# The bias row of a fused attention and MLP kernel as one matmul in place of three

## The chip, the cores and the metric

The kernel runs on one core of one Trainium2 chip. The metric is the device time of one execution in microseconds (us). Times are given as the median of several runs. One more execution is recorded by the hardware profiler, and the numbers about single instructions come from that one.

## The reference

Two stages are computed. The first is a gated linear attention over 4 batches, 8 heads, 768 steps and a head width of 48: a state is decayed, a product of key and value is added, and the query reads it. The second is an MLP with a squared ReLU over the 3072 rows of 384 that come out of it.

```python
for t in range(S):
    state = alpha[:, :, t, :, None] * state + einsum('bhd,bhe->bhde', k[:, :, t], v[:, :, t])
    y[:, :, t] = einsum('bhd,bhde->bhe', q[:, :, t], state)
x = y.transpose(0, 2, 1, 3).reshape(B * S, H * D)
h = x @ w_in                       # 384 -> 2048
r = maximum(h, 0.0)
g = s * (r * r) + b
out = g @ w_out                    # 2048 -> 384
```

Since `b` is one number, `b` times the column sums of `w_out` is the same row for all 3072 outputs. This is the bias row: 384 numbers, which are added to each row of `(s * r * r) @ w_out`.

## The kernel before

The 3072 rows are cut into 24 blocks of 128 (`n` from 0 to 23, six for each batch). For each block the kernel forms the decays (`ln`, `cum_pe`, `cum_act`), scales queries and keys (`qb_mul`, `kb_mul`), transposes them (`tr`, `qk_copy`), forms the scores (`amat`) and masks them (`mask`), and forms the attention's output (`y_pe`, `y_act`). It carries the state on with `pst_pe`, `t1` and `sd`. The output is transposed (`xt_pe`, `xt_act`), goes through the first matrix in four quarters (`mp`, with `rl` and `sq` behind each), and through the second, again in four quarters (`o_pe`, then `o_out`). Matmul inputs are bf16; sums are fp32.

The program is straight-line code. Each step is an event with a position on a scale of 8 per block; events are sorted by position and issued in that order. Each engine takes its own instructions in this order, and a semaphore holds an instruction back until what it needs is there. The position thus sets the order in each engine's queue and not a time.

PSUM, where matmuls put their results, has eight banks, and each is one tile here: `ct_ps`, two `a_ps`, `y_ps`, `p_ps`, two `h_ps` and `o_ps`. The output of the attention takes columns 0 to 383 of `y_ps`; the state's product takes columns 0 to 383 of `p_ps`. From block 11 on, the scores of odd blocks are written into all 512 columns of `y_ps` and `p_ps`, those of even blocks into the two `a_ps`.

The bias row is made in three steps. `colsum` adds up the pieces of `w_out` on VectorE (up to position 101.3), and `bias_sum` folds the two halves of that into `cs_sb[:, 0]`, 128 partitions by 384 columns (position 103.3). `bias_row` then sums over the partitions: a matmul with a matrix of ones in fp32 puts the same sums into all 128 partitions, and a ScalarE activation scales them by `b` and puts them into `bias_w`. Before the change this is done for 128 columns at a time: part 0 goes into columns 384 to 511 of `y_ps` at position 105.5, part 1 into the same columns of `p_ps` at 105.6, and part 2 again into `y_ps` at 121.5.

The events around positions 105.5 and 121.5, in their order:

```
103.9   y_pe 13, pst_pe 13, y_act 13        119.9   y_pe 15, pst_pe 15, y_act 15
104.05  o_pe 12 (quarter 0)                 120.05  o_pe 14 (quarter 0)
104.74  tr 15                               120.74  tr 17
104.95  t1 13, sd 13                        120.95  t1 15, sd 15
105.5   bias_row part 0 (y_ps)              121.5   bias_row part 2 (y_ps)
105.6   bias_row part 1 (p_ps)
105.65  o_pe 12 (quarter 1)                 121.65  o_pe 14 (quarter 1)
105.71  qk_copy 15                          121.71  qk_copy 17
105.89  xt_pe 13, xt_act 13                 121.89  xt_pe 15, xt_act 15
106.17  amat 14, then amat 15 (106.35)      122.17  amat 16, then amat 17 (122.35)
```

`bias_w` is first read at position 125.3. The results of the first 14 blocks are kept in SBUF until then (`o_out` puts them into `keep_sb`, and `add_bias` adds the row later); those of later blocks get it as they leave PSUM.

The lines of the profile for these steps: L210 and L211 are matmul and activation of `bias_row`, L206 is `bias_sum`, L329 the transposes, L341 their copy, L362 the scores, L371 the masks, L467 and L476 the attention's output, L498 its evacuation, L489 the state's product and L550 (or L548) `t1`, L528 and L535 the transposed output and its copy, L574 the first matrix, L587 and L594 ReLU and square, L605 the second matrix.

Of the kernel before, what the change touches and what calls it, by code (L numbers as in the profile page):

```python
# [10 lines left out]
AF = mybir.ActivationFunctionType  # L11
# [3 lines left out]
def kernel(  # L15
# [12 lines left out]
    nc = tc.nc  # L28
# [28 lines left out]
    y_ps = ps.tile([128, 512], FP32, name="y_ps")  # L57
    p_ps = ps.tile([128, 512], FP32, name="p_ps")
# [19 lines left out]
    ones_f = sb.tile([128, 128], FP32, name="ones_f")  # L78
    sb_row = sb.tile([1, 2], FP32, name="sb_row")
    sb_col = sb.tile([128, 2], FP32, name="sb_col")  # L80
    s_col, b_col = sb_col[:, 0:1], sb_col[:, 1:2]
# [36 lines left out]
    cs_sb = sb.tile([128, 2, d_model], FP32, name="cs_sb")  # L118
    bias_w = sb.tile([128, d_model], FP32, name="bias_w")
# [85 lines left out]
    def bias_sum():  # L205
        nc.vector.tensor_tensor(out=cs_sb[:, 0], in0=cs_sb[:, 0], in1=cs_sb[:, 1], op=ALU.add)  # L206

    def bias_row(i):
        part, c = (y_ps, p_ps, y_ps)[i][:, 384:512], slice(128 * i, 128 * i + 128)
        nc.tensor.matmul(out=part, lhsT=ones_f, rhs=cs_sb[:, 0, c], start=True, stop=True)  # L210
        nc.scalar.activation(out=bias_w[:, c], in_=part, func=AF.Copy, scale=b_col)  # L211

    def spread():
        nc.tensor.matmul(out=p_ps[:, 510:512], lhsT=ones_f[0:1], rhs=sb_row, start=True, stop=True)
# [489 lines left out]
    for s in range(2):  # L704
        nc.vector.memset(mask_p[s], 0.0)
        for b in range(2):
            part = mask_p[s][64 * b : 64 * b + 64]
            nc.gpsimd.affine_select(
                out=part,
                in_=part,  # L710
# [17 lines left out]
    def at(pos, fn, *args):  # L728
        events.append((pos, len(events), fn, args))
# [55 lines left out]
    for i in range(3, 8):  # L785
        at(69.3 + 8 * (i - 3), colsum, i)
    at(103.3, bias_sum)
    for i in range(3):
        at((105.5, 105.6, 121.5)[i], bias_row, i)
    for n in range(NKEEP):  # L790
        at(125.3 + 4.55 * n, add_bias, n)
        at(126.2 + 4.55 * n, store, n, keep_sb[n])
# [15 lines left out]
    for n in range(4, NBLK):  # L808
        p = 8 * n
        f = max(0.0, min((n - 5) / 3.0, 1.0))  # L810
        c, t, a = 9.0 + 5.8 * f, 5.8 + 5.0 * f, 3.4 + 4.5 * f
# [59 lines left out]
```

## Time and profile before

| | |
|---|---|
| median of 3 runs | 185.96 us (185.91 to 186.97) |
| profiled execution: time, span | 186.9 us, 185.1 us |
| mean granted TensorE clock | 0.991 |
| TensorE matmul busy | 178.9 us, 97% of the span |
| VectorE busy | 142.4 us, 77% |
| ScalarE busy | 122.8 us, 66% |
| GpSimd busy | 58.9 us, 32% |

The span is what the profiler sees from the first to the last instruction; 1.8 us of the profiled execution lie around it. In the rows of the profile, PE is TensorE's matmuls and PEld its weight loads, DVE is VectorE, ACT ScalarE, POOL GpSimd, and SPq the queue from which SyncE issues transfers. L210 is line 210 of the kernel. A row names the tile that is written, then those that are read (`out<-in`), with the numbers of ring buffers left out. Matmuls overlap: a record's end includes the tail of the pipeline, so the distance between the starts of two matmuls, and not the duration of one, is what a matmul takes of the array's time. The chain is followed back from the last instruction to what released each step; its pieces do not overlap.

### The profile page before, as it was taken

To read this page: it belongs to the slowest core of one execution; us is meant where nothing else is said; L and a number is where in the kernel's file an instruction comes from. 1 tells how busy PE (TensorE), PEld (TensorE's weight loads), DVE (VectorE), ACT (ScalarE), POOL (GpSimd) and SP (SyncE) were. 2 spreads that over 40 slices of the span, in tenths; PEclk is the share of its full clock that TensorE was granted. 3 is DMA by queue.
4 is the path that set the end of the run, shared out by engine and by line. 5 is a ranking of instruction groups with operands and counts; after the bars stand their busy time and mean duration, and the time that the engine had idled before them with its cause. 6 is when DMAs were issued, how large, how long until landed. Compare 5 with 4: busy or idle time off the path is not lost.

```text
span 185.1 us, 6233 instructions
## 1 busy us (share of the span) xinstructions
PE 178.9 (97%) x2510; PEld 143.7 (78%) x2510; DVE 142.4 (77%) x301; ACT 122.8 (66%) x255; POOL 58.9 (32%) x97
## 2 busy tenths in 40 slices
PE   7988999999999999999999999999999999999993
PEld 2556999866698777787888778878878878878893
DVE  7688878866657588987888976689789799886541
ACT  3885897976678957656766756856746746734750
POOL 7437470011330625042505343242202442333000
PEclk9996999999999999999999999999999999999999
DMA  5998989989478989892976563934896944224212
GB/s 155 312 317 307 270 235 387 317 158 208 76 153 151 211 163 189 165 175 43 172 138 123 104 121 78 192 74 124 157 207 142 189 135 132 66 66 149 65 52 76
DMA packets 105262, 30.33 MB, mean 164 GB/s; under 512 B 98435, under 2 KB 103698, under 8 KB 105234
## 3 DMA queue, kind: packets, MB, share of 16 engines
q1 hardware_dynamic: 105230, 29.94, 69.5%
q8 instruction: 19, 0.31, 0.7%
q14 instruction: 9, 0.07, 0.1%
q10 hardware_dynamic: 4, 0.00, 0.0%
HBM read 25.19 MB, written 4.74 MB: 162 GB/s over the span
## 4 chain that ended last, share of the span: by engine, by line
PE 83%; DMA 4%; DVE 3%; ACT 3%; SPq 2%; issue 1%; POOL 1%; ACTq 0%; POOLq 0%; DVEq 0%
PE h_ps L574 27%; PE o_ps L605 26%; PE ct_ps L329 4%; PE h_ps L605 3%; DMA al_sb<-in_alpha_dram 3%; PE a_ps L574 2%; PE a_ps L362 2%; PE y_ps L476 2%; PE ct_ps L574 2%; SPq L152 2%; PE h_ps L528 2%; DMA v_sb<-in_v_dram 2%; PE o_ps L574 2%; PE ct_ps L256 1%; PE a_ps L631 1%
## 5 line engine op out<-in xcount | busy, mean ns | idle before, releaser
L574 PEld LDWEIGHTS <-w_in_bf 128*128 128x128 bf16 x1152 | 67.5, 98 | 4.4 <-issue 0.2
L587 ACT ACTIVATE r_sb<-h_ps 128x512 bf16<-128x512 f32 x79 | 46.9, 603 | 30.7 <-PE h_ps L574 29.0
L605 PE MATMUL o_ps<-w_out_bf,gt_all 128*128 128x384 bf16 x320 | 64.0, 326 | 0.0
L574 PE MATMUL h_ps<-xd_all,w_in_bf 128*128 128x128 bf16 x948 | 60.3, 219 | 0.0
L560 POOL TENSOR_TENSOR sd_sb<-t_sb,blast 48x192 bf16<-48x192 f32 x40 | 25.7, 642 | 86.2 <-DVE t_sb L550 58.8
L594 DVE TENSOR_TENSOR gt_all<-r_sb 128x512 bf16<-128x512 bf16 x96 | 40.7, 441 | 15.8 <-ACT r_sb L587 15.6
L605 PEld LDWEIGHTS <-gt_all 128*128 128x128 bf16 x368 | 32.6, 98 | 15.3
L251 POOL CAST v_bf<-v_sb 128x384 bf16<-128x384 f32 x23 | 14.6, 646 | 23.5 <-DMA v_sb<-in_v_dram 21.4
L318 DVE TENSOR_TENSOR kb_sb<-k_sb,bi_sb 128x384 bf16<-128x384 f32 x24 | 14.5, 605 | 7.4 <-ACT bi_sb L269 7.4
L321 DVE TENSOR_TENSOR qb_sb<-q_sb,b_sb 128x384 bf16<-128x384 f32 x24 | 13.5, 564 | 2.1 <-ACT b_sb L270 1.6
L535 ACT ACTIVATE xd_all<-h_ps 128x384 bf16<-128x384 bf16 x19 | 9.5, 502 | 8.0 <-PE h_ps L528 7.9
L564 POOL TENSOR_TENSOR sc_sb<-t_sb,blast 112x384 f32<-112x384 f32 x16 | 14.3, 895 | 1.3
L240 ACT ACTIVATE la_sb<-al_sb 128x384 bf16<-128x384 f32 x24 | 12.5, 529 | 2.7 <-DVE blast L721 2.3
L498 ACT ACTIVATE y_bf<-y_ps 128x384 bf16<-128x384 f32 x22 | 10.9, 498 | 3.5 <-PE y_ps L476 3.1
L371 DVE TENSOR_TENSOR am_a<-a_ps,mask 128x512 bf16<-128x512 f32 x13 | 8.9, 687 | 5.0 <-PE a_ps L362 4.9
L341 DVE COPY qkT<-ct_ps 112x1024 bf16<-112x1024 bf16 x16 | 11.0, 685 | 2.3 <-PE ct_ps L329 2.1
L329 PEld LDWEIGHTS <-qb_sb 128*112 128x112 bf16 x96 | 8.3, 133 | 4.0 <-DVE qb_sb L321 2.5
L269 ACT ACTIVATE bi_sb<-ct_ps 128x384 f32<-128x384 f32 x19 | 9.3, 489 | 2.1 <-PE ct_ps L256 2.0
L371 DVE TENSOR_TENSOR am_b<-a_ps,mask 128x512 bf16<-128x512 f32 x13 | 8.9, 682 | 1.7 <-PE a_ps L362 1.7
L270 ACT ACTIVATE b_sb<-ct_ps 128x384 f32<-128x384 f32 x19 | 9.4, 497 | 0.0
L656 DVE TENSOR_TENSOR w_in_st<-w_in_st,bias_w 128x384 f32<-128x384 f32 x14 | 8.3, 593 | 0.0
L329 PEld LDWEIGHTS <-kb_sb 128*112 128x112 bf16 x96 | 7.4, 133 | 0.7 <-DVE kb_sb L318 0.2
(145 smaller groups left out, 256.9 us busy)
## 6 DMA issues: line engine op xcount, KB each, us to landing
al_sb<-in_alpha_dram SPq DMA_DIRECT2D x20, 192.0 KB, 2.9
q_sb<-in_q_dram SPq DMA_DIRECT2D x20, 192.0 KB, 4.2
k_sb<-in_k_dram SPq DMA_DIRECT2D x20, 192.0 KB, 8.1
v_sb<-in_v_dram SPq DMA_DIRECT2D x20, 192.0 KB, 3.6
w_in_st<-in_moe_w_in_dram SPq DMA_DIRECT2D x4, 768.0 KB
w_out_st<-in_moe_w_out_dram SPq DMA_DIRECT2D x4, 768.0 KB
out_dram<-w_in_st SPq DMA_DIRECT2D x10, 192.0 KB
out_dram<-out_sb SPq DMA_DIRECT2D x5, 192.0 KB, 2.2
```

The costliest lines, as they stand in the source:

```text
L240: nc.scalar.activation(out=la_sb[n % 2][:, :, 0:48], in_=raw("al", n), func=AF.Ln)
L251: nc.gpsimd.tensor_copy(out=v_bf[n % 4], in_=raw("v", n))
L318: nc.vector.tensor_tensor(out=kb_sb[n % 4][:, :, 0:48], in0=raw("k", n), in1=bi_sb[n % 2], op=ALU.mult)
L321: nc.vector.tensor_tensor(out=qb_sb[n % 2][:, :, 0:48], in0=raw("q", n), in1=b_sb[n % 3], op=ALU.mult)
L329: nc.tensor.transpose(out=t_bank(n, x if n in pair_of else None)[0:112, x, p, :], in_=t.rearrange("a h d -> a (h d)")[:, 128 * p : 128 * p ...
L371: nc.vector.tensor_tensor(out=am_sb[e][n % 2], in0=a_bank(n)[e], in1=mask4, op=ALU.mult)
L560: nc.gpsimd.tensor_tensor(out=sd[r, :, d], in0=t1_sb[r, :, d], in1=bl[r].to_broadcast([48, NP, 48]), op=ALU.mult)
L564: nc.gpsimd.tensor_tensor(out=sc_sb[0:112], in0=t1_sb[0:112], in1=bl[0:112].to_broadcast([112, NP, 96]), op=ALU.mult)
L574: nc.tensor.matmul(out=hp[:, jj * C : (jj + 1) * C], lhsT=w_in_bf[:, kk, 128 * j : 128 * (j + 1)], rhs=xd_sb[n][:, kk], start=(kk == 0), s ...
L587: nc.scalar.activation(out=rs, in_=room((g, u)), func=AF.Relu)
L594: nc.vector.tensor_tensor(out=gt_sb[g][:, u * 512 : (u + 1) * 512], in0=rs, in1=rs, op=ALU.mult)
L605: nc.tensor.matmul(out=op[:, 0:d_model], lhsT=gt_sb[n][:, j * C : (j + 1) * C], rhs=w_out_bf[:, j, :], start=(j == 0), stop=(j == NJ - 1),)
```

## The change

The sums over the partitions are formed by one matmul of 384 columns into columns 0 to 383 of `y_ps`, the place of the attention's output, and one activation takes them to `bias_w`. It stands at position 105.5; the events at 105.6 and 121.5 are gone.

```diff
-    def bias_row(i):
-        part, c = (y_ps, p_ps, y_ps)[i][:, 384:512], slice(128 * i, 128 * i + 128)
-        nc.tensor.matmul(out=part, lhsT=ones_f, rhs=cs_sb[:, 0, c], start=True, stop=True)
-        nc.scalar.activation(out=bias_w[:, c], in_=part, func=AF.Copy, scale=b_col)
+    def bias_row():
+        nc.tensor.matmul(out=y_ps[:, 0:384], lhsT=ones_f, rhs=cs_sb[:, 0], start=True, stop=True)
+        nc.scalar.activation(out=bias_w, in_=y_ps[:, 0:384], func=AF.Copy, scale=b_col)
...
     at(103.3, bias_sum)
-    for i in range(3):
-        at((105.5, 105.6, 121.5)[i], bias_row, i)
+    at(105.5, bias_row)
```

## The prediction

> **What bounds the kernel now.** I read the page first: the share of each engine, the granted clock, and the chain that ended last.
>
> ```profile
> span 185.1 us, 6233 instructions
> PE 178.9 (97%) x2510; PEld 143.7 (78%) x2510; DVE 142.4 (77%) x301; ACT 122.8 (66%) x255; POOL 58.9 (32%) x97
> PEclk9996999999999999999999999999999999999999
> PE 83%; DMA 4%; DVE 3%; ACT 3%; SPq 2%; issue 1%; POOL 1%; ACTq 0%; POOLq 0%; DVEq 0%
> ```
>
> TensorE is busy for 97% of the span, holds 83% of the chain, and runs at full clock in every slice but one early on. The change lies after 104 us, so the question is whether TensorE waits for anything between there and the end. Next I read the table of waits, for TensorE's matmuls and then for its weight loads, from 106 us to the end.
>
> ```profile
> PE p_ps L210 <- DVE t_sb L550: 0.3, 1, 0.3
> ...
> PEld p_ps L210 <- DVE t_sb L550: 0.5, 1, 0.5
> PEld L329 <- DVE qb_sb L321: 0.3, 1, 0.3
> ```
>
> The columns are total us, times, longest us. In 80 us the matmul side waits once, and that wait belongs to the code being changed: the second part of the bias row (L210, into `p_ps`) waits for VectorE's state sum `t1` (L550), which reads the other columns of the same bank. The wait is thus kept for the bank, not for the columns. Everything else arrives in time, so an instruction taken from TensorE's queue here should bring the end forward by the time it held the queue.
>
> **The change part by part.** The timeline around 105.5 us has all of the first two parts. Columns are start, duration, engine, line, operation, and in brackets the idle time before with what ended it.
>
> ```profile
> 105.24 0.39 PE L329 MATMUL ct_ps<-ident,kb_sb 128*112 128x128 bf16 x4
> 105.41 0.30 PEld L210 LDWEIGHTS y_ps<-cs_sb,ones_f 128*128 128x128 f32 x2
> 105.47 0.44 PE L210 MATMUL y_ps<-cs_sb,ones_f 128*128 128x128 f32 x2
> 105.63 0.55 DVE L550 TENSOR_TENSOR t_sb<-p_ps,sc_sb 112x384 f32<-112x384 f32 x1
> 105.94 0.37 ACT L211 ACTIVATE bias_w<-y_ps,sb_col 128x128 f32<-128x128 f32 x1 [0.80 <-PE y_ps L210]
> 106.10 0.68 DVE L341 COPY qkT<-ct_ps 112x1024 bf16<-112x1024 bf16 x1
> 106.23 0.49 PE L210 MATMUL p_ps<-cs_sb,ones_f 128*128 128x128 f32 x2 [0.33 <-DVE t_sb L550]
> 106.56 0.81 PE L605 MATMUL o_ps<-w_out_bf,gt_all 128*128 128x384 bf16 x4
> 107.58 0.49 ACT L535 ACTIVATE xd_all<-h_ps 128x384 bf16<-128x384 bf16 x1 [0.45 <-PE h_ps L528]
> 107.70 0.22 PE L362 MATMUL y_ps<-qkT 48*128 48x128 bf16 x1
> ```
>
> One fp32 matmul of the source is two instructions. The output product behind both parts (L605) starts at 106.56, which is 106.56 - 105.47 = 1.09 us after the first part began.
>
> The third part stands alone, without a stall. The chain in order of time gives its cost (start, length, what):
>
> ```profile
> 120.14 0.45 PE ct_ps L329 x8
> 120.58 0.28 PE y_ps L210 x2
> 120.86 0.65 PE o_ps L605 x4
> ...
> 122.99 1.34 PE h_ps L574 x24
> ```
>
> It holds 0.28 us of the chain, with TensorE's work packed on both sides. All of that goes: **-0.28 us**. Three parts at this price are 0.84 us, and the stall is what else the 1.09 us holds, 1.09 - 0.56 = 0.53 us by starts (the table shows 0.3 for the matmuls, because a record's end includes the tail that the next matmul overlaps, and 0.5 for the weight loads).
>
> What is added is an fp32 matmul of 384 columns, of which the trace has none. Its nearest rows are the 128-column calls:
>
> ```profile
> L210 PEld LDWEIGHTS y_ps<-cs_sb,ones_f x4: 190/191/192, 105.4 to 120.5; 128*128 128x128 f32 x4
> L210 PE MATMUL y_ps<-cs_sb,ones_f x4: 275/302/328, 105.5 to 120.6; 128*128 128x128 f32 x4
> L210 PE MATMUL p_ps<-cs_sb,ones_f x2: 275/326/377, 106.2 to 106.4; 128*128 128x128 f32 x2
> ```
>
> The second instruction of the `p_ps` call ends at 106.23 + 0.49 = 106.72 and lasts 0.275, so it starts at 106.445, and the next matmul starts at 106.56: a pass over 128 columns holds the array for 0.115 us. A bf16 matmul of 128 columns takes 1.34/24 = 0.056 us of the chain (L574), so fp32 costs twice that per pass. The bf16 matmul of 384 columns takes 0.65/4 = 0.1625 us (L605). Two fp32 passes over 384 columns should then take 2 x 2 x 0.1625 = **0.65 us**. The first pass of a 128-column call is longer, 0.28 - 0.115 = 0.165 us, which I put down to the second weight load (0.19 us); behind a first pass of 0.325 us that load is covered. The bounds are the bf16 rate below, 2 x 0.1625 = 0.33 us, and three calls above, 0.84 us. I take 0.65, since it has the measured fp32 rate and the measured width.
>
> The output product then starts at 105.47 + 0.65 = 106.12 instead of 106.56: **-0.44 us**. The bounds make it -0.76 to -0.25.
>
> The Trainium skill, "TensorE: Matmul & The Clock Gate", section "Back-to-back issue gap", gives a warm matmul N/2.4 + 2.5 ns, and "Perfetto Trace Analysis", section "Engine Utilization", halves the output rate for the fp32 low-high form. An estimate from both pages is 2 x (320 + 2.5) = 645 ns for the wide call and 6 x (107 + 2.5) = 657 ns for the three narrow ones. By that rule the merging alone is worth 12 ns, and nearly the whole gain would be the stall, about 0.5 us in all. The trace agrees for the second pass (115 ns against 109) and not for the first (165 ns); the measured 0.28 a call decides.
>
> ScalarE's side: three activations of 0.367 us become one over 384 columns. Widening it is priced by two PSUM readers of ScalarE:
>
> ```profile
> L211 ACT ACTIVATE bias_w<-y_ps,sb_col x2: 367/367/367, 105.9 to 120.9; 128x128 f32<-128x128 f32 x2
> ...
> L587 ACT ACTIVATE r_sb<-h_ps 128x512 bf16<-128x512 f32 x68 | 40.6, 604 | 30.4 <-PE h_ps L574 28.8
> ...
> L498 ACT ACTIVATE y_bf<-y_ps 128x384 bf16<-128x384 f32 x16 | 8.0, 501 | 1.7 <-PE y_ps L476 1.7
> ```
>
> 128 more columns cost 604 - 501 = 103 ns, so the new one takes 367 + 2 x 103 = 573 ns (between 0.49, the narrower price of L498, and 3 x 0.367 = 1.10). Nothing on the path pays for it: ScalarE sits idle 0.80 us before the first part, and behind it in its queue is the copy of the transposed block (L535), which waits for TensorE in any case.
>
> **What the wide evacuation can hold up.** The next writer of the bank of `y` is the score product of the following block (L362 into `y_ps`, 107.70, about 107.26 after the change). The wide matmul ends with its tail of 0.16 us (0.275 - 0.115) at 106.28, ScalarE starts 0.03 later as it does now (105.91 to 105.94), and ends near 106.88. That leaves about 0.4 us, less the handoff. If the matmul takes longer, writer and reader move together; only an activation beyond about 0.95 us would reach the score product, so its upper bound of 1.10 would cost 0.15 us. The other input of that product, VectorE's copy (L341), ends at 106.78: 0.48 us early. The `t1` for which the second part waited ends at 106.18, and its next user on TensorE, the score product into `p_ps`, comes at about 107.27. So the stall has no successor. In front of the new matmul nothing new is waited for: it needs the evacuation of `y` and the sum of the bias, as the first part did, and that part started right behind the transposes (L329). No DMA is added or moved, and the queues of SP and POOL are passed by nothing.
>
> **Sum.** -0.44 - 0.28 = -0.72 us, with bounds -1.04 and -0.53. Against the profiled execution that is a span of 185.1 - 0.7 = 184.4 us and a time of 186.9 - 0.7 = 186.2 us. The profiled execution is 0.9 us above the median of the runs (185.96, from 185.91 to 186.97), so the same difference put on the median gives **185.25 us**, own range 184.9 to 185.45.
>
> **Rivals.**
>
> *The gain is taken back later.* TensorE arrives earlier everywhere behind 106 us, and VectorE is nearly full: in the stretch from 150 to 170 us it is busy 18.29 of 20 us.
>
> ```profile
> 150.00:170.00 20.00, 20.00 (x286) 16.56 (x285) 18.29 (x38) 11.69 (x24) 6.84 (x10) 1.00 0.30 89
> ```
>
> At one place the chain already shows the seam:
>
> ```profile
> 107.87 0.05 PE y_ps L362
> ...
> 149.49 0.18 PE y_ps L362
> ```
>
> It takes 0.18 us there against 0.05 at 107.87, and VectorE's copy for that block (L341 below) ends just then, at 148.71 + 0.68 = 149.39. If VectorE's pace were its own, TensorE would wait 0.72 us longer at that seam and the kernel would end at 185.96. Against it: VectorE's unbroken run up to that copy begins with a wait for ScalarE, which waited for TensorE.
>
> ```profile
> 144.61 0.45 DVE L594 TENSOR_TENSOR gt_all<-r_sb 128x512 bf16<-128x512 bf16 x1 [1.08 <-ACT r_sb L587]
> 145.28 0.42 DVE L594 TENSOR_TENSOR gt_all<-r_sb 128x512 bf16<-128x512 bf16 x1 [0.22 <-ACT r_sb L587]
> ...
> 148.71 0.68 DVE L341 COPY qkT<-ct_ps 112x1024 bf16<-112x1024 bf16 x1
> ```
>
> So the run starts earlier when TensorE does. Half a loss would be 185.6. Chance 0.18 for 185.45 to 185.96.
>
> *The change does not do what it says: the merged matmul is no cheaper than three.* Then the call takes 0.84, the output product starts at 106.31, and the sum is -0.25 - 0.28 = -0.53: 185.43, the upper edge of the forecast. If the score product also met the late evacuation (0.15), it is 185.6. By the rule of the Trainium skill above the time would lie here as well, at 185.96 - 0.5 = 185.46. Chance 0.08.
>
> *Slower: a wide fp32 pass doesn't overlap.* If each 128 columns of a pass cost their whole record of 0.275 us, the wide call would hold TensorE from 105.47 for 6 x 0.275 = 1.65 us. The output product would start at 107.12, 0.56 us later than before; with the third part's 0.28 gone that is +0.28, or 186.24. It decides from a call of 0.65 + 0.72 = 1.37 us on. The 0.115 us from a second pass to the next matmul, seen twice, speaks against it. Chance 0.06.
>
> **How the numbers follow.** The forecast has 0.68, the rivals 0.18, 0.08 and 0.06. The range of 184.9 to 186.1 reaches from the lower bound of the forecast over the whole of the first two rivals, with a little room above for scatter, and leaves out most of the slower one. A measurement of this kernel can tell about 1% from no change, which is 184.1 or 187.8 us. None of the cases reaches either; I leave 0.04 on each side for what I have not seen, and 0.92 for within 1%.
>
> **What would show it.** On the changed kernel's timeline: two fp32 matmul instructions of 384 columns from about 105.5 us, with the output product (L605) 0.65 us behind the first; no wait for `t_sb` among TensorE's; one activation of about 0.57 us, over before the score product into `y_ps`; no fp32 matmul near 120 us; and the same step of the chain 0.44 us earlier at 107 us and 0.72 us earlier from 121 us to the end. The prediction is wrong if that lead shrinks on the way, which would put the seam at the place where it shrinks, or if the wide call's two instructions start more than 0.4 us apart.

## The result and the profile after

| | before | after |
|---|---|---|
| median of 22 runs each, side by side | 186.39 us | 185.85 us |
| ratio | | 0.996, 95% interval 0.9944 to 0.9976 |
| span of the profiled execution | 185.1 us | 183.9 us |
| TensorE matmul busy | 178.9 us | 177.7 us |

The ratio is a gain of 0.75 us (0.45 to 1.04) on 186.39; -0.72 had been forecast. The two medians lie only 0.54 us apart; four runs of before are above 187.5 us and no run of after is above 186.24. The gain is clear of no change and well under 1%. The forecast of 185.25 was put on a median of three runs; the median of 22 runs of before is 0.43 us higher, and this, more than the change, is why the time itself lies 0.6 us above the forecast. That is outside the forecast's own range (184.9 to 185.45) and in the stretch that the first rival had claimed, although what that rival tells of did not happen.

The two spans differ by 1.2 us, more than the change gave. The table of stretches shows why. Columns are the stretch, its length, busy time and count of PE, PEld, DVE, ACT and POOL, the granted clock, and the share and rate of DMA. The first fence is before, the second after.

```profile
0.00:20.00 20.00, 17.16 (x230) 11.04 (x231) 15.81 (x46) 13.21 (x32) 10.71 (x27) 0.91 0.95 281
```

```profile
0.00:20.00 20.00, 16.90 (x242) 10.67 (x243) 16.89 (x46) 13.96 (x34) 10.91 (x28) 1.00 1.00 293
```

In the profiled execution of before, the clock was 0.91 in the first 20 us, where the two programs are alike. I therefore measure from an instruction ahead of the change: the **tail** runs from the state's part of `y` of block 13 to VectorE's last instruction. (The expectations below call this the end of that instruction; all their numbers, and mine here, take its start.) Its two ends before and, in the second fence, after:

```profile
103.83 0.34 PE L467 MATMUL y_ps<-sd_sb,qkT 112*128 112x96 bf16 x4
...
182.29 0.36 DVE L640 TENSOR_TENSOR out_sb<-a_ps,bias_w 128x192 f32<-128x192 f32 x1 [0.30 <-PE a_ps L631]
```

```profile
103.27 0.34 PE L466 MATMUL y_ps<-sd_sb,qkT 112*128 112x96 bf16 x4
...
181.06 0.36 DVE L639 TENSOR_TENSOR out_sb<-a_ps,bias_w 128x192 f32<-128x192 f32 x1 [0.30 <-PE a_ps L630]
```

The tail is 182.29 - 103.83 = 78.46 us before and 181.06 - 103.27 = 77.79 after, so the change itself is worth **-0.67 us** in the trace. Another 0.56 us of the difference of the spans lies ahead of the tail (103.83 against 103.27). The timeline of after around the new matmul (lines of the kernel are one lower than before from L209 on):

```profile
104.85 0.30 PEld L209 LDWEIGHTS y_ps<-cs_sb,ones_f 128*128 128x128 f32 x2
104.91 0.86 PE L209 MATMUL y_ps<-cs_sb,ones_f 128*128 128x384 f32 x2
105.54 0.68 DVE L340 COPY qkT<-ct_ps 112x1024 bf16<-112x1024 bf16 x1
105.61 0.81 PE L604 MATMUL o_ps<-w_out_bf,gt_all 128*128 128x384 bf16 x4
105.81 0.58 ACT L210 ACTIVATE bias_w<-y_ps,sb_col 128x384 f32<-128x384 f32 x1 [1.23 <-PE y_ps L209]
106.75 0.22 PE L361 MATMUL y_ps<-qkT 48*128 48x128 bf16 x1
```

The **call**, from the start of the first bias matmul to the start of the output product behind it, takes 105.61 - 104.91 = 0.70 us; before it was 1.09 with the stall. Among TensorE's waits from 100 us on, `t_sb` is gone. What is left is the wait for `qb_sb`, which was there before, and an idle of the weight loads with no releaser:

```profile
PEld L328 <- DVE qb_sb L320: 0.3, 1, 0.3
PEld L604 <- issue: 0.2, 1, 0.2
```

In the chain, the transposes at the old place of part 2 are followed directly by the output product:

```profile
119.19 0.45 PE ct_ps L328 x8
119.63 0.65 PE o_ps L604 x4
...
148.27 0.18 PE y_ps L361
```

The lead against before, counted from the start of the tail, is 0.39 us at the scores of block 15 (107.70 - 103.83 against 106.75 - 103.27). It is 0.67 behind the old place of part 2, and the same 0.67 at the end. The seam near 149 us is still 0.18 us long.

### The profile page after: what moved, and what is told of

Same layout as the page of the kernel before. It is cut to its first block, busy times and chain, and to the rows that moved or that the text cites. A ratio compares the mean times of both kernels' runs of the same rounds, so it can differ in the third digit from the quotient of the medians.

```text
span 183.9 us, 6223 instructions
## 1 busy us (share of the span) xinstructions
PE 177.7 (97%) x2506; PEld 142.3 (77%) x2506; DVE 143.4 (78%) x301; ACT 122.6 (67%) x253; POOL 60.3 (33%) x97
## 4 chain that ended last, share of the span: by engine, by line
PE 90%; ACT 4%; DVE 3%; issue 1%; POOL 1%; ACTq 0%; POOLq 0%; DVEq 0%
PE h_ps L573 29%; PE o_ps L604 28%; PE ct_ps L328 5%; PE h_ps L604 3%; PE a_ps L573 2%; PE a_ps L361 2%; PE o_ps L229 2%; PE y_ps L475 2%; PE ct_ps L573 2%; PE h_ps L527 2%; PE ct_ps L255 2%; PE o_ps L573 2%; PE y_ps L466 1%; PE a_ps L630 1%; PE a_ps L604 1%; PE p_ps L488 1%
## 5 line engine op out<-in xcount | busy, mean ns | idle before, releaser
L559 POOL TENSOR_TENSOR sd_sb<-t_sb,blast 48x192 bf16<-48x192 f32 x40 | 26.9, 672 | 85.8 <-DVE t_sb L549 57.8
L250 POOL CAST v_bf<-v_sb 128x384 bf16<-128x384 f32 x23 | 15.4, 678 | 21.2 <-DMA v_sb<-in_v_dram 19.2
L563 POOL TENSOR_TENSOR sc_sb<-t_sb,blast 112x384 f32<-112x384 f32 x16 | 13.8, 864 | 1.3
```

The source lines that it names most:

```text
L250: nc.gpsimd.tensor_copy(out=v_bf[n % 4], in_=raw("v", n))
L559: nc.gpsimd.tensor_tensor(out=sd[r, :, d], in0=t1_sb[r, :, d], in1=bl[r].to_broadcast([48, NP, 48]), op=ALU.mult)
L563: nc.gpsimd.tensor_tensor(out=sc_sb[0:112], in0=t1_sb[0:112], in1=bl[0:112].to_broadcast([112, NP, 96]), op=ALU.mult)
```

## Experiments

Each kernel was timed beside the kernel before, in runs of the same chip; ratios are to those. The tail and the call are read from each trace. They are the finer measure: an interval of a ratio is about 0.2% to either side, or 0.4 us. A tail comes from one execution, and how far it scatters from one to the next was not measured; but what each trace below shows around the bias row, calls and waits, adds up to the change of its tail within 0.03 us.

**Three narrow matmuls at one place.** It isolates the width.

```diff
-        nc.tensor.matmul(out=y_ps[:, 0:384], lhsT=ones_f, rhs=cs_sb[:, 0], start=True, stop=True)
+        for i in range(3):
+            c = slice(128 * i, 128 * i + 128)
+            nc.tensor.matmul(out=y_ps[:, c], lhsT=ones_f, rhs=cs_sb[:, 0, c], start=True, stop=True)
```

> The place and the single activation of the changed kernel, but three matmuls of 128 columns side by side in the bank of y in place of the wide one. It isolates the width. Two distances are read from the trace: the call, from the start of the first bias matmul to the start of the output product behind it (1.09 us before, with the stall; 0.70 after), and the tail, from the start of the state's part of y of block 13 to the end of VectorE's last instruction (182.29 - 103.83 = 78.46 us before, 181.06 - 103.27 = 77.79 after). My prediction's price of 0.28 us a call makes the call 3 x 0.28 = 0.84 and the tail 77.93. A rival reading of the changed kernel's trace is that only the first weight load of the whole row is exposed (0.05 us) and each narrow pass costs 0.115: call 6 x 0.115 + 0.05 = 0.74, tail 77.83. By the rule of the back-to-back gap the call is 0.66 to 0.71 and the tail as after.

The grouped rows of this kernel's bias line, and its timeline:

```profile
L211 PEld LDWEIGHTS y_ps<-cs_sb,ones_f x6: 190/192/192, 105.1 to 105.7; 128*128 128x128 f32 x6
L211 PE MATMUL y_ps<-cs_sb,ones_f x6: 275/275/328, 105.2 to 105.8; 128*128 128x128 f32 x6
...
105.19 0.89 PE L211 MATMUL y_ps<-cs_sb,ones_f 128*128 128x128 f32 x6
...
105.91 0.81 PE L606 MATMUL o_ps<-w_out_bf,gt_all 128*128 128x384 bf16 x4
```

The ends of its tail:

```profile
103.55 0.34 PE L468 MATMUL y_ps<-sd_sb,qkT 112*128 112x96 bf16 x4
...
181.37 0.36 DVE L641 TENSOR_TENSOR out_sb<-a_ps,bias_w 128x192 f32<-128x192 f32 x1 [0.30 <-PE a_ps L632]
```

The call takes 105.91 - 105.19 = 0.72 us, and the tail 181.37 - 103.55 = 77.82. The ratio is 0.9975 (0.9957 to 0.9994). Only the first of the six records is longer than 275 ns. So the width is worth 0.02 to 0.03 us: three narrow matmuls in a row cost 0.72 and not 3 x 0.28 = 0.84. The price of 0.28 belongs to a call that stands alone behind the transposes.

**The stall alone.** The kernel before, with part 1 behind the next quarter of the output product.

```diff
-        at((105.5, 105.6, 121.5)[i], bias_row, i)
+        at((105.5, 105.66, 121.5)[i], bias_row, i)
```

> The kernel before, with part 1 of the bias row one event later, behind the second quarter of the output product of block 12, so that the state sum it waits for is done. It isolates the stall. My theory: the stall of 0.53 us goes with nothing in its place but a short wait of the scores of block 15 for the later evacuation of that part (0 to 0.15 us): tail 77.93 to 78.08 against 78.46, ratio to before 0.997 to 0.998. Rival, the gain of the change comes from the merging and not from the stall: tail about 78.4.

In this execution the tail begins at 107.20. The granted clock was 1.00 throughout it.

```profile
107.20 0.34 PE L467 MATMUL y_ps<-sd_sb,qkT 112*128 112x96 bf16 x4
...
110.19 0.37 ACT L211 ACTIVATE bias_w<-p_ps,sb_col 128x128 f32<-128x128 f32 x1 [0.50 <-PE p_ps L210]
110.49 0.22 PE L362 MATMUL y_ps<-qkT 48*128 48x128 bf16 x1
110.61 0.21 PE L362 MATMUL p_ps<-qkT 48*128 48x128 bf16 x1
...
185.19 0.36 DVE L640 TENSOR_TENSOR out_sb<-a_ps,bias_w 128x192 f32<-128x192 f32 x1 [0.30 <-PE a_ps L631]
```

The tail is 77.99 us, 0.47 less than before; the ratio is 0.9977 (0.9954 to 1.0), whose interval just reaches no change. One event's place gives 0.47 of the 0.67 us, with nothing merged. A little of the stall comes back as the short wait that was expected: the score product into `p_ps` starts 0.12 us behind its neighbour and not 0.01 as before, when the activation that reads this bank is done (110.19 + 0.37 = 110.56).

**The wide matmul in the other bank.** `p_ps` in place of `y_ps`.

```diff
-        nc.tensor.matmul(out=y_ps[:, 0:384], lhsT=ones_f, rhs=cs_sb[:, 0], start=True, stop=True)
-        nc.scalar.activation(out=bias_w, in_=y_ps[:, 0:384], func=AF.Copy, scale=b_col)
+        nc.tensor.matmul(out=p_ps[:, 0:384], lhsT=ones_f, rhs=cs_sb[:, 0], start=True, stop=True)
+        nc.scalar.activation(out=bias_w, in_=p_ps[:, 0:384], func=AF.Copy, scale=b_col)
```

> The changed kernel with the wide matmul in the bank of the state's product in place of the bank of y. It isolates the choice of the bank. My theory: TensorE waits for the state sum of block 13 as part 1 did, 0.76 us behind the point at which the matmul could start; the call costs 0.70 as after, and the tail is 77.79 + 0.76 = 78.55 us, 0.1 us longer than before. Rival, the merging is what gains: tail 77.8.

```profile
106.72 0.91 PE L209 MATMUL p_ps<-cs_sb,ones_f 128*128 128x384 f32 x2 [0.60 <-DVE t_sb L549]
...
107.47 0.81 PE L604 MATMUL o_ps<-w_out_bf,gt_all 128*128 128x384 bf16 x4
```

The ends of its tail:

```profile
104.31 0.34 PE L466 MATMUL y_ps<-sd_sb,qkT 112*128 112x96 bf16 x4
...
182.93 0.36 DVE L639 TENSOR_TENSOR out_sb<-a_ps,bias_w 128x192 f32<-128x192 f32 x1 [0.30 <-PE a_ps L630]
```

The wait is back. The tail is 182.93 - 104.31 = 78.62 us, 0.16 longer than before, and the ratio 1.0011 (0.999 to 1.0033). Merged in this bank, the row gains nothing. The call takes 0.75 us here and not 0.70: TensorE had run empty, and nothing hides any of the first weight load.

**No bias row at all.** The row is zero here, so the bias is left out of the output.

```diff
-    at(105.5, bias_row)
+    at(118.35, nc.vector.memset, bias_w, 0.0)
```

> The changed kernel without the matmul and the activation of the bias row; the row is set to zero by VectorE instead, at a place where VectorE waits, so the bias is left out of the output. It measures what the row costs TensorE in all and whether a further gain is taken back later. My theory: all of the call's 0.70 us reaches the end, tail 77.09 us, ratio to before 0.992 to 0.993. Rival, VectorE takes part of the lead back behind 145 us: tail between 77.1 and 77.79, with waits of TensorE for VectorE near 148 us.

```profile
105.59 0.68 DVE L340 COPY qkT<-ct_ps 112x1024 bf16<-112x1024 bf16 x1
...
106.32 0.23 PEld L361 LDWEIGHTS <-qkT 48*128 48x128 bf16 x8 [0.23 <-DVE qkT L340]
```

The ends of its tail:

```profile
103.31 0.34 PE L466 MATMUL y_ps<-sd_sb,qkT 112*128 112x96 bf16 x4
...
180.65 0.36 DVE L639 TENSOR_TENSOR out_sb<-a_ps,bias_w 128x192 f32<-128x192 f32 x1 [0.30 <-PE a_ps L630]
```

The tail is 180.65 - 103.31 = 77.34 us and not 77.09; the ratio is 0.9934 (0.9912 to 0.9956). Of the call's 0.70 us, 0.45 reach the end. The rest is, within 0.02 us, a new wait of 0.23 us of the scores of block 15 for VectorE's copy, right behind the place of the row and not near 148 us. The prediction had put this copy 0.48 us early, and 0.70 - 0.48 = 0.22. That this fits so well is in part luck: in the changed kernel the copy ends 0.53 us before the scores (106.22 against 106.75), and the handoff takes 0.05 of that (106.27 to 106.32 here).

**The row at a calmer place.** Behind an output product of block 13, ten positions later (the expectation says nine).

```diff
-    at(105.5, bias_row)
+    at(115.64, bias_row)
```

> The changed kernel with the bias row nine positions later, behind an output product of block 13 and ahead of the transposes of block 16, where the bank of y is free for some 5 us. The matmul ahead of the call is then one of 384 columns and not a transpose of 128. Theory A, the 0.05 us by which the first pass is longer than the second (0.375 against 0.325 in the changed kernel) is the first fp32 weight load, which a longer matmul ahead would cover: first pass 0.325 to 0.33, call 0.65, tail 77.74 us. Theory B, it is a fixed price of a first fp32 pass: first pass 0.375, call 0.70, tail 77.79. Nothing is gained by the later evacuation in either case.

```profile
L209 PE MATMUL y_ps<-cs_sb,ones_f x2: 486/486/486, 113.1 to 113.4; 128*128 128x384 f32 x2
...
106.59 0.22 PEld L361 LDWEIGHTS <-qkT 48*128 48x128 bf16 x8 [0.23 <-DVE qkT L340]
...
113.09 0.81 PE L209 MATMUL y_ps<-cs_sb,ones_f 128*128 128x384 f32 x2
...
113.74 0.39 PE L328 MATMUL ct_ps<-ident,qb_sb 128*112 128x128 bf16 x4
```

Both passes now have the same 486 ns (542 and 486 in the changed kernel), and the call is 113.74 - 113.09 = 0.65 us. Theory A holds: the 0.05 is the first weight load, which a wide matmul ahead covers. But neither theory foresaw the tail, 181.57 - 103.59 = 77.98 us. At 105.5 the row fills time in which TensorE would wait for the copy anyway, and away from there this wait of 0.23 us shows: 77.79 - 0.05 + 0.23 = 77.97. The ratio is 0.9978 (0.9964 to 0.9992).

**The row in bf16.** `cs_bf` is a new bf16 tile, and `warm` is a bf16 tile of ones that the kernel has.

```diff
-        nc.vector.tensor_tensor(out=cs_sb[:, 0], in0=cs_sb[:, 0], in1=cs_sb[:, 1], op=ALU.add)
+        nc.vector.tensor_tensor(out=cs_bf, in0=cs_sb[:, 0], in1=cs_sb[:, 1], op=ALU.add)
...
-        nc.tensor.matmul(out=y_ps[:, 0:384], lhsT=ones_f, rhs=cs_sb[:, 0], start=True, stop=True)
+        nc.tensor.matmul(out=y_ps[:, 0:384], lhsT=warm[:, 0], rhs=cs_bf, start=True, stop=True)
```

> The changed kernel with the column sums written as bf16 and multiplied with a bf16 matrix of ones: one pass at the bf16 rate in place of two at the fp32 rate. My theory: the call falls from 0.70 to 0.16 us (0.65/4 for the bf16 matmul of 384 columns), and the tail to 77.25 us, ratio to before 0.993 to 0.994. Rival, VectorE takes part of it back later: tail between 77.25 and 77.79.

```profile
105.20 0.33 PE L210 MATMUL y_ps<-cs_bf,warm 128*128 128x384 bf16 x1
...
105.36 0.81 PE L605 MATMUL o_ps<-w_out_bf,gt_all 128*128 128x384 bf16 x4
...
105.83 0.68 DVE L341 COPY qkT<-ct_ps 112x1024 bf16<-112x1024 bf16 x1
...
106.56 0.23 PE L362 MATMUL y_ps<-qkT 48*128 48x128 bf16 x1
```

The call is 0.16 us and the tail 180.88 - 103.56 = 77.32, 0.07 longer than forecast. The copy ends at 106.51, and the scores, which could have started near 106.50, start at 106.56: the same wait, of which the row still fills the most. The ratio is 0.993 (0.9911 to 0.9949). The tail is 0.47 us shorter than that of the changed kernel and no longer than without any row (77.34): in bf16 the row costs the end nothing that these traces show. The price is that the column sums are rounded to bf16.

**The row one event later.** The evacuation then ends later, and the scores stay.

```diff
-    at(105.5, bias_row)
+    at(105.66, bias_row)
```

> The changed kernel with the bias row one event later, behind the second quarter of the output product of block 12. The evacuation of the bank of y then ends 0.65 us later, while the scores of block 15, which write this bank, stay where they are. My theory: matmul's end 1.46 us behind the point at which the row starts in the changed kernel, activation from 1.49 to 2.07, and the first score product into the bank of y is ready at 1.80: TensorE waits about 0.3 us for the activation, and the tail is 77.79 + 0.3 - 0.05 = 78.0 to 78.1 us. Rival, the scores don't wait, or something else moves up: tail 77.75.

```profile
107.38 0.21 PE L361 MATMUL y_ps<-qkT 48*128 48x128 bf16 x1 [0.17 <-ACT bias_w L210]
107.38 0.22 PEld L361 LDWEIGHTS <-qkT 48*128 48x128 bf16 x7 [0.30 <-issue]
```

The tail is 181.70 - 103.61 = 78.09 us, as worked out; the ratio is 0.9984 (0.9969 to 0.9999). The scores wait for the activation.

**The activation twice.**

```diff
         nc.scalar.activation(out=bias_w, in_=y_ps[:, 0:384], func=AF.Copy, scale=b_col)
+        nc.scalar.activation(out=bias_w, in_=y_ps[:, 0:384], func=AF.Copy, scale=b_col)
```

> The changed kernel with the activation of the bias row done twice (the same result written twice), so that the bank of y is read until 106.88 us in place of 106.39. My theory: the first score product of block 15 into that bank, at 106.75 now, waits for it: 0.15 to 0.2 us, tail 77.95 to 78.0 us. Rival, the evacuation has more room than I worked out: tail 77.79.

```profile
106.04 0.58 ACT L210 ACTIVATE bias_w<-y_ps,sb_col 128x384 f32<-128x384 f32 x1 [1.23 <-PE y_ps L209]
...
106.65 0.58 ACT L211 ACTIVATE bias_w<-y_ps,sb_col 128x384 f32<-128x384 f32 x1
106.75 0.28 PEld L362 LDWEIGHTS <-qkT 48*128 48x128 bf16 x9
...
107.28 0.21 PE L362 MATMUL y_ps<-qkT 48*128 48x128 bf16 x1
```

The second activation starts 0.61 us behind the first, where I had taken 0.49, and the tail is 181.61 - 103.50 = 78.11 us, 0.32 above the changed kernel and 0.11 above the upper end that I had given. The room for the evacuation is thus about 0.3 us (0.61 - 0.32), as worked out. The ratio, 0.9998 (0.9985 to 1.0012), makes this kernel 0.04 us shorter than the one before, where the tails say 0.35. Part of the difference goes with the clock: over the runs in which it was granted at 0.997 or more, the medians are 186.26 and 186.51 us, 0.25 apart. The rest stays open.

## Why the prediction was right, point by point

- *The time.* 185.85 us lies in the range of 184.9 to 186.1 only because that range was drawn over the rivals too, and that part is luck: it made up for the low median of three runs. What was right is the step, -0.72 forecast and -0.67 in the trace.
- *TensorE's queue is the bound, and what leaves it reaches the end.* Right for this change: -0.67 us in the trace against the -0.72 of the sum, with the lead unchanged from 121 us to the end. The row left out shows how near the limit was: the next 0.70 us bring only 0.45.
- *The stall of 0.53 us goes and has no successor.* Right, though its size was nearer 0.48 (below). Moving one part alone gave 0.47 us, and the other bank brought the wait back. That the wait is kept for the bank and not the columns rests on the one wait in the table, where the matmul wrote columns 384 to 511 and `t1` read 0 to 383. The run with `p_ps` can't add to it, since its matmul writes the very columns that `t1` reads.
- *Part 2's 0.28 us goes.* Right: transposes and output product are neighbours there now.
- *The wide call costs 0.65 us.* Mis-sized by 0.05: it took 0.70, and this is all that separates -0.67 from -0.72. I had put the longer first pass down to the second weight load, which a wide first pass covers. It is the first load of the call that is exposed behind a short transpose; behind a wide matmul the call did take 0.65. The two instructions start 0.37 us apart (the pair ends at 104.91 + 0.86 = 105.77, and the second lasts 0.486), just inside the 0.4 that the prediction had named as a sign of being wrong.
- *Three narrow calls cost 0.84 us.* Wrong as a price of three in a row, which took 0.72. The estimate from the Trainium skill ("TensorE: Matmul & The Clock Gate", section "Back-to-back issue gap") made the width worth 12 ns, and 20 to 30 ns were measured: for the merging itself, the rule was nearer than my price of 0.28 a call. Its total of 0.5 us was too low: that section calls the formula the gap of an isolated matmul, with no budget for weight loads, and here a first load was exposed three times. The rival by which the merged matmul is no cheaper than three was thus nearly right about the merging and wrong about the price: both cost about 0.7, not 0.84.
- *So the 0.67 us are made up otherwise than I had them.* The matmuls of part 1 began 0.48 us later than the array was free (105.75 to 106.23). The first passes of the three old calls were 0.05, 0.10 and 0.05 us too long, against one of 0.05 now, which is 0.15. The rest, about 0.04, is the width and rounding. What gained is the place of the row, in one piece and in a bank that is free at that time.
- *The evacuation takes 573 ns and has about 0.4 us of room.* 581 ns, with 106.75 - 106.39 = 0.36 us before the handoff; the two runs with a later end of it made the scores wait as computed.
- *VectorE might take the gain back at 149 us.* It did not: that seam moved along with TensorE. The place where VectorE limits is the copy for block 15, whose 0.48 us of room the prediction had worked out but had not made a rival.

## What to carry to other kernels

When an engine's queue is packed, price a step by what its place does to the queue: the wait it brings, its first weight load, and what it covers. Here merging three matmuls was worth 0.02 to 0.03 us, and taking one of them out of a bank that was still being read some 0.5. Write down the slack of each input behind the change, since the smallest of them is how much more can be gained at that place.

## What was not expected

An fp32 weight load of 190 ns costs 0.05 us when a 128-column bf16 transpose stands ahead of it, 0.10 us when the array is idle, and nothing behind a matmul of 384 columns or another fp32 pass. These prices fit one account, which no run tests by itself: the load delays the array by 0.10 us, less what the matmul ahead of it holds the array (0.45/8 = 0.056 us for a transpose, 0.11 for an fp32 pass over 128 columns, 0.16 for 384 columns in bf16). And a piece of work on TensorE, the busiest engine, can be partly free: at position 105.5, 0.23 us of the call's 0.70 filled a wait that would otherwise be there.
